# Strided attention in tiles of 36 tokens over four parts of TensorE's array, and weight slots at multiples of 128 bytes

## The chip, the cores and the metric

The kernel runs on one core of one Trainium2 chip. The metric is the device time of one execution in microseconds (us); the time of a kernel is the median of its runs. TensorE (PE) multiplies matrices, VectorE (DVE) and ScalarE (ACT) work elementwise, GpSimd (POOL) builds masks, SyncE (SP) issues nearly all DMA transfers.

## The reference

Inputs q, k, v have the shape (4, 8, 576, 64): batch, heads, tokens, head dimension, in float32. Heads 0 to 3 are local, heads 4 to 7 strided:

```
rel = pos[:, None] - pos[None, :]
mask_local   = (rel >= 0) & (rel < 32)
mask_strided = (rel >= 0) & (pos[None, :] % 32 == pos[:, None] % 32)
scores = where(mask, (q @ k.T) / 8, -1e9);  attn = exp(scores - max) / (sum + 1e-9);  attn @ v
```

The 2304 tokens of the result (4 batches of 576, 512 channels) go through two layers: `g = h * tanh(softplus(h))` with `h = x @ w_in` (512 to 2048) and `g @ w_out` back to 512; then `max(x @ w1, x @ w2, x @ w3) @ w_out` with an inner size of 768. The weights come as 8-byte numbers; the kernel turns them into a high and a low 4-byte part itself.

In strided attention a token sees only tokens with the same number modulo 32, so the 576 tokens fall into 32 residues of 18 tokens. A tile takes some whole residues; the mask lets a token see only its own residue's earlier tokens.

## The kernel before, in words

**Planner.** `build_plan` describes all work as small pieces with an engine, an estimated cost, the buffers that it reads and writes, and a rank. `Plan.run` plays a list schedule over the engines and `settle` repeats it forward and backward; the order found is emitted as it is. So every change of a piece can move the order of all of the others. Where PE would idle the planner puts filler matmuls (`fill`, L839) in.

**Attention.** There are 16 groups, one for each batch and pair of heads (`hp`); `hp` 0 and 1 are local, 2 and 3 strided. q and k of batch 0 are loaded early and transposed on PE (L355, copied at L368 and L370); the others are loaded as 128-byte pieces and transposed by DVE (L329), which writes the tokens of strided heads in the order of the residues. v comes by `load_v`; strided: six transfers a group, in 256-byte pieces (L834). `unit` (L377) handles 3 local tiles of 64 queries and 96 keys, or 4 (at the end 3) strided tiles of 3 residues: 54 queries and keys, 11 tiles a group, the last with 36. For each unit, in one PSUM bank from start to end: scores of both heads (PE, L413; head 0 in the rows 0 to 53 of the bank, head 1 from row 64 on), mask and scale (DVE, L426), row maximum (DVE, L432), for each tile an exponential with its sum (ACT, L438), guard, reciprocal and normalising (DVE, L445 to L451), a transpose of each tile (PE, L458), copy to `pt` (ACT, L463), product with v (PE, L471), and the result as a high part (ACT, L489) and the rest (DVE, L493) written to `x` at every 32nd token. Five banks (`ATT_BANKS`) go round among the units. The tiles `s`, `st` and `pt` are rings of 5, 8 and 3.

**First layer.** Products of 288 tokens with the first four chunks of w_in (L516, "raw", into `hr`) need the attention of their batch alone and lie among the attention units of the later batches; the last two blocks of tokens (8 of the 32 units) must follow the last attention unit. Then L543 multiplies by the first four chunks of w_out, and for five blocks of tokens (four of 512, one of 256) the chunks f = 4 to 15 of w_in (L516) and w_out (L543) follow. **Second layer:** for each block and each f = 0 to 5, w1 to w3 (L590) and w_out2 (L615; here the weights are the moving operand). A matmul with high and low parts is done as three passes over four chunks, so a group has 12 instructions.

**Slots.** Converted weights (4 KB in each partition) lie in 5 slots `a`, 11 slots `x` (laid over attention's buffers once these are closed) and 8 slots `y` (in the right-hand region, laid over `hr`). The right-hand region is laid out from the top down: first one block with `ident`, `edge` (an unused tile of 32 bytes), `wt`, `h` and `ev`, and below it, in turn, the early buffers, `hr` and the y slots. As laid out, every a and x slot begins at a multiple of 128 bytes and every y slot 64 bytes past one (the lowest at 168128 = 1313 x 128 + 64). By the order in which slots are freed, the y slots hold the chunks f = 10 to 13 of w_in and w_out in the first layer, and in the second six of the 18 chunks of w1 to w3 and two of the six of w_out2.

Of the kernel before, what the change touches and what calls it, by code (L numbers as in the profile page):

```python
# [19 lines left out]
P = 128  # L20
# [14 lines left out]
RES = 3  # L35
ATT_BANKS = ("a0", "a1", "a2", "acc1", "acc2")
RAW_BANKS = ("h0", "acc3")
# [152 lines left out]
def build_plan(k, B, H, S, D, DM, FF, FF2, wide):  # L190
# [110 lines left out]
    unit_tiles = {True: ((0, 1, 2), (3, 4, 5), (6, 7, 8)), False: ((0, 1, 2, 3), (4, 5, 6, 7), (8, 9, 10))}  # L301
    per_batch = 3 * H // 2
# [8 lines left out]
    def attention():  # L311
        n = 0
        for i, (b, hp) in enumerate(pairs):
            local = hp < 2
            r = i % 2
            rv = i if i < RING["v"] + 2 else i % RING["v"]
            rk0 = unit_rank(n)
            lr = rk0 - 8 if b else -200 + i
            if not b:
                early_qk(i, b, hp, local, r, rk0, lr)  # L320
            for nm in ("q", "k") if b else ():
                for g in range(4):
                    add("qk_load", "sp", S * PACKET[128], (lambda g=g, nm=nm, b=b, hp=hp, r=r: k.load_qk(nm, g, b, hp, k.raw(nm, r))),
                        writes=[("raw", nm, r, g)], rank=lr)

                def tr(nm=nm, r=r, local=local):
                    t = k.qkT(nm, r)
                    tv = t.rearrange("p (j r) -> p j r", r=STRIDE) if local else t.rearrange("p (r j) -> p j r", j=NJ)
                    nc.vector.transpose(out=tv, in_=k.raw(nm, r))  # L329

                add("tr", "dve", 669, tr, reads=[("raw", nm, r, g) for g in range(4)], writes=[("qT", nm, r)], rank=rk0 - 0.5)
            vparts = k.v_parts(hp)
            for j in range(vparts):
                v_cost = PACKET[256] * (LK * (2 if j == 0 else NL - 1) if local else NJ * (NS - (j % RES == RES - 1)))
                add("v_load", "sp", v_cost, (lambda j=j, b=b, hp=hp, rv=rv: k.load_v(j, b, hp, k.v(rv))),
                    writes=[("v", rv, j_) for j_ in range(j, 2 * RES, vparts)], rank=lr + 0.5)
            for u, tiles in enumerate(unit_tiles[local]):
                unit(n, i, u, tiles, b, hp, local, r, rv)
                n += 1
            if i == H // 2 - 1:  # L340
                add("hrpool", "dve", 0, k.open_hrpool, writes=[("earlypool",)], rank=-1)

    def early_qk(i, b, hp, local, r, rk0, lr):
# [5 lines left out]
        for j in range(2):  # L349
            for nm in ("q", "k"):  # L350
# [9 lines left out]
                def copy(nm=nm, j=j, tag=tag):  # L360
                    t, src = k.qkT(nm, r), k.bank(tag)[:, :half]
                    if local:
                        t = t[:, half * j:half * (j + 1)]
                    else:
                        t = t.rearrange("p (r j) -> p r j", j=NJ)[:, :, NJ // 2 * j:NJ // 2 * (j + 1)]
                        src = src.rearrange("p (j r) -> p r j", r=STRIDE)
# [10 lines left out]
    def unit(n, i, u, tiles, b, hp, local, r, rv):  # L377
# [5 lines left out]
        tag = ATT_BANKS[n % len(ATT_BANKS)]  # L383
        bk = ("bank", tag)
# [24 lines left out]
        for j, tl in enumerate(tiles):  # L409
            def scores(j=j, tl=tl):  # L410
                kw = LK if local else width(tl)
                for h in range(2):
                    nc.tensor.matmul(  # L413
                        ps()[LQ * h:LQ * h + width(tl), j * K:j * K + kw],
                        lhsT=cols("q", h, tl), rhs=cols("k", h, tl), start=True, stop=True,
                    )
            add("scores", "pe", 212 if local else 142, scores, reads=[("qT", "q", r), ("qT", "k", r)], writes=[bk], rank=rk, cols=4 * (K if local else width(tl)))

        def mask():
# [4 lines left out]
            else:  # L424
                m = k.m_first[:, 1, :].unsqueeze(1).broadcast_to([rows, nt, K])
            nc.vector.scalar_tensor_tensor(  # L426
                out=sv(), in0=ps()[:rows, :nt * K].rearrange("p (n c) -> p n c", c=K),
# [6 lines left out]
        add("mask", "dve", dve(nt * K), mask, reads=[bk], writes=[sb, *sk], rank=rk)  # L434
# [31 lines left out]
        for j, tl in enumerate(tiles):  # L466
# [9 lines left out]
            add("av", "pe", 160, av, reads=[pk] + [("earlypool",)] * (rv >= RING["v"]) + [("v", rv, j_) for j_ in range(2 * RES)], writes=[bk], rank=rk, cols=8 * width(tl) * K / P)  # L476
# [19 lines left out]
        add("a_lo", "dve", dve(nt * M), lo, reads=[bk, xhi, *at], writes=[xlo], rank=rk)  # L496

# [187 lines left out]
def sparse_attention_moe_kernel(  # L685
# [34 lines left out]
    upper.tile([P, 8], F32, name="edge")  # L720
# [16 lines left out]
    s_t = many(atc, "s", [P, 3 * LK])  # L737
    st_t = many(atc, "st", [P, 8])
# [3 lines left out]
    v_t = many(atc, "v", [P, 2, NS, D])  # L742
    v_t += [early_pool.tile([P, 2, NS, D], F32, name=f"v{i}") for i in range(RING["v"], RING["v"] + 2)]
# [8 lines left out]
    def build_masks():  # L752
# [8 lines left out]
        for h in range(2):  # L761
            half = m_res[LQ * h:LQ * (h + 1)].rearrange("p (r j) -> p r j", j=NJ)
            select(half, [[-NJ, RES], [-1, NJ]], 0, 1)
            select(half, [[NJ, RES], [0, NJ]], NJ - 1, -1)
# [52 lines left out]
    def load_v(j, b, hp, t):  # L817
# [12 lines left out]
        else:  # L830
            h, r = divmod(j, RES)
            vr = v[b, 2 * hp + h].rearrange("(j r) d -> j r d", r=STRIDE)
            n = len(range(r, STRIDE, RES))
            nc.sync.dma_start(out=t[NJ * r:NJ * (r + 1), h, :n, :], in_=vr[:, r::RES, :])  # L834
# [18 lines left out]
    with tc.manual_schedule():  # L853
# [5 lines left out]
        build_masks()  # L859
        for emit in order:  # L860
# [30 lines left out]
```

## Time and profile before

| | |
|---|---|
| median of 3 runs | 807.09 us (807.07 to 807.59) |
| profiled execution | 807.78 us; span of its instructions 806.0 us |
| PE busy | 797.0 us (99%), 5017 matmul instructions; 9 tenths or more in 39 of 40 slices |
| DVE busy | 360.7 us (45%) |
| ACT busy | 320.9 us (40%) |
| POOL busy | 4.4 us |
| DMA | 59.66 MB, 119,690 packets, of which 91,984 under 512 bytes |
| granted TensorE clock | 1.00 throughout |

The span reaches from the first to the last instruction. Busy time counts the time in which an instruction of the engine is under way; matmuls are pipelined and overlap, so that a busy PE may still have room. The chain of waits follows the run back from its last instruction to whatever released each step; its pieces say how long a group of instructions held up the end. A small float32 matmul of the attention appears as two PE instructions.

### The profile page before, as it was taken

The numbers are of one execution on the slowest core, as the hardware profiler recorded it, in microseconds if no ns is written. First come the engines' busy times: TensorE is split into PE (matmuls) and PEld (weight loads), VectorE is DVE, ScalarE is ACT, GpSimd is POOL, SyncE is SP. The second block draws the span as 40 slices with busy tenths as digits, with TensorE's granted clock in tenths as the row PEclk, the third lists the DMA queues.
The fourth block names the chain that finished last, engine by engine and source line by source line (L and its number), as shares of the span: only waits on it lengthen the run. The fifth ranks groups of instructions, "written<-read, shape, count | busy, mean of one in ns | idle before, by whom it ended". The sixth has DMA issues, their size and how long they took to land.

```text
span 806.0 us, 12605 instructions
## 1 busy us (share of the span) xinstructions
PE 797.0 (99%) x5017; PEld 669.3 (83%) x5017; DVE 360.7 (45%) x769; ACT 320.9 (40%) x839; POOL 4.4 (1%) x22
## 2 busy tenths in 40 slices
PE   9999999999999999999999999999999999999998
PEld 7878888988888888888888899888888888888897
DVE  6988886895931311311321179981212211122222
ACT  5978878997732322312322257630110110110111
POOL 2000000000000000000000000000000000000000
PEclk9999999999999999999999999999999999999999
DMA  9877750944900100100010079200100010010010
GB/s 206 157 152 132 135 102 22 349 148 170 326 0 1 53 0 1 53 0 1 1 52 0 1 227 322 105 1 0 53 1 0 16 38 1 0 53 1 0 53 27
DMA packets 119690, 59.66 MB, mean 74 GB/s; under 512 B 91984, under 2 KB 110416, under 8 KB 119632
## 3 DMA queue, kind: packets, MB, share of 16 engines
q1 hardware_dynamic: 118448, 58.57, 26.5%
q8 instruction: 39, 0.64, 0.3%
q10 hardware_dynamic: 1184, 0.30, 0.2%
q14 instruction: 19, 0.16, 0.1%
HBM read 49.41 MB, written 9.44 MB: 73 GB/s over the span
## 4 chain that ended last, share of the span: by engine, by line
PE 92%; DMA 3%; ACT 2%; DVE 2%; issue 1%; SPq 0%; DVEq 0%; ACTq 0%
PE bank_acc L543 24%; PE bank_a L590 21%; PE bank_a L516 13%; PE bank_acc L615 9%; PE bank_h L516 7%; PE bank_h L590 7%; PE bank_acc L516 3%; PE bank_a L413 2%; PE bank_a L471 1%; DMA wslot<-in_moe_w_dram 1%; PE bank_a L458 1%; DMA wslot<-in_moe_w_out_dram 1%; PE bank_acc L413 1%; ACT s L438 1%; PE bank_acc L471 1%; PE bank_acc L458 1%
## 5 line engine op out<-in xcount | busy, mean ns | idle before, releaser
L543 PE MATMUL bank_acc<-g,wslot 128*128 128x512 f32 (+1 forms) x960 | 205.4, 370 | 1.4 <-ACT g L537 1.0
L543 PEld LDWEIGHTS bank_acc<-g,wslot 128*128 128x128 f32 x960 | 168.3, 188 | 33.7 <-ACT g L537 1.2
L590 PE MATMUL bank_a<-x,wslot 128*128 128x512 f32 (+1 forms) x816 | 174.7, 369 | 0.0
L590 PEld LDWEIGHTS bank_a<-x,wslot 128*128 128x128 f32 x816 | 142.3, 188 | 26.9
L538 DVE TENSOR_TENSOR g<-h,g 128x512 fp32r<-128x512 f32 (+1 forms) x80 | 51.1, 639 | 194.8 <-ACT g L537 194.8
L516 PE MATMUL bank_a<-x,wslot 128*128 128x512 f32 (+1 forms) x540 | 117.2, 369 | 0.0
L516 PEld LDWEIGHTS bank_a<-x,wslot 128*128 128x128 f32 x540 | 94.5, 188 | 17.9
L599 DVE TENSOR_TENSOR h<-bank_a,h 128x512 f32<-128x512 f32 (+1 forms) x46 | 29.2, 635 | 138.9 <-PE bank_a L590 138.9
L615 PE MATMUL bank_acc<-wslot,g 128*128 128x512 f32 x324 | 78.8, 391 | 0.0
L516 PE MATMUL bank_h<-x,wslot 128*128 128x288 f32 (+2 forms) x372 | 74.5, 339 | 0.0
L615 PEld LDWEIGHTS bank_acc<-wslot,g 128*128 128x128 f32 x324 | 60.5, 188 | 12.8
L535 ACT ACTIVATE h<-bank_a 128x512 f32<-128x512 f32 (+1 forms) x45 | 25.0, 555 | 109.8 <-PE bank_a L516 109.8
L516 PEld LDWEIGHTS bank_h<-x,wslot 128*128 128x128 f32 x372 | 58.5, 188 | 7.4
L601 ACT ACTIVATE g<-h 128x512 fp32r<-128x512 f32 (+1 forms) x30 | 17.7, 589 | 116.1 <-DVE h L599 116.1
L590 PE MATMUL bank_h<-x,wslot 128*128 128x512 f32 (+1 forms) x264 | 58.8, 371 | 0.0
L438 ACT ACTIVATE s<-s,st 118x54 f32<-118x54 f32 (+1 forms) x160 | 55.5, 352 | 7.2 <-DVE st L432 6.9
L590 PEld LDWEIGHTS bank_h<-x,wslot 128*128 128x128 f32 x264 | 46.7, 188 | 9.0
L537 ACT CAST g<-h 128x512 fp32r<-128x512 f32 (+1 forms) x80 | 46.3, 579 | 4.5 <-PE bank_acc L543 2.7
L253 ACT ACTIVATE wt<-wslot 128x512 f32<-128x512 f32 x56 | 37.9, 678 | 22.7 <-DVE wslot L281 9.7
L277 ACT CAST wslot<-wt 128x512 fp32r<-128x512 f32 x56 | 34.5, 621 | 15.3 <-DVE wt L267 15.1
L281 DVE TENSOR_TENSOR wslot<-wt,wslot 128x512 fp32r<-128x512 f32 x56 | 38.6, 692 | 3.4 <-ACT wslot L277 3.4
L596 ACT COPY h<-bank_a 128x512 f32<-128x512 f32 (+1 forms) x22 | 12.0, 548 | 69.8 <-PE bank_a L590 69.8
(71 smaller groups left out, 680.4 us busy)
## 6 DMA issues: line engine op xcount, KB each, us to landing
wslot<-in_moe_w_out_dram SPq DMA_DIRECT2D x22, 512.0 KB
wslot<-in_moe_w_dram SPq DMA_DIRECT2D x18, 512.0 KB
wslot<-in_moe_w_in_dram SPq DMA_DIRECT2D x16, 512.0 KB
out_dram<-wt SPq DMA_DIRECT2D x18, 256.0 KB
x2p<-ev SPq DMA_DIRECT2D x16, 256.0 KB
ev<-x2p SPq DMA_DIRECT2D x16, 256.0 KB
rawq<-in_q_dram SPq DMA_DIRECT2D x48, 72.0 KB
rawk<-in_k_dram SPq DMA_DIRECT2D x48, 72.0 KB
```

Source lines behind the costliest of these rows:

```text
L253: nc.scalar.mul(k.wt(r2).bitcast(F32), k.words(slot)[1].bitcast(F32), 2.0 ** -111)
L277: nc.scalar.copy(out=k.open_slot(slot)[:, 0, :], in_=k.wt(r2).bitcast(F32))
L281: nc.vector.tensor_tensor(out=s[:, 1, :], in0=k.wt(r2).bitcast(F32), in1=s[:, 0, :], op=ALU.subtract)
L438: nc.scalar.activation(sv()[:, j, :], sv()[:, j, :], AF.Exp, bias=mx()[:, j:j + 1], accum_out=dn()[:, j:j + 1],)
L516: nc.tensor.matmul(k.bank(hb)[:, :n], lhsT=wap(("in", f), a, c), rhs=k.x[:, q, c, t0:t0 + n], start=(c == 0 and m == 0), stop=(c == KC - 1 ...
L535: add(name, "act", act(n, psum=not stored), lambda: nc.scalar.activation(Hh(), src(), AF.Mish, scale=W_SCALE), reads=sread, writes=[HK], r ...
L537: add("gh", "act", act(n), lambda: nc.scalar.copy(out=g()[:, 0, :n], in_=Hh()), reads=[HK], writes=[G0], rank=s)
L538: add("gl", "dve", dve(n), lambda: nc.vector.tensor_tensor(out=g()[:, 1, :n], in0=Hh(), in1=g()[:, 0, :n], op=ALU.subtract), reads=[HK, G0 ...
L543: nc.tensor.matmul(k.bank(f"acc{c}")[:, :n], lhsT=wap(("out", f), a, c), rhs=g()[:, q, :n], start=(first and m == 0), stop=(last and m == 2),)
L590: nc.tensor.matmul(k.bank(hb)[:, :n], lhsT=wap((w_, f), a, c), rhs=k.x[:, q, c, t0:t0 + n], start=(c == 0 and m == 0), stop=(c == KC - 1 a ...
L599: add("m2", "dve", dve(n), (lambda hb=hb: nc.vector.tensor_tensor(out=m_(), in0=k.bank(hb)[:, :n], in1=m_(), op=ALU.max)), reads=[("bank", ...
L615: nc.tensor.matmul(k.bank(ab)[:], lhsT=k.g(rg)[:, a, c * P:(c + 1) * P], rhs=t[:, q, :], start=(f == 0 and m == 0), stop=(f == F2C - 1 and ...
```

## The change

Strided units get a function of their own, `pair_unit`. A tile now has 2 residues (36 tokens), 16 tiles a group. A tile of the first half (residues a * 16 + n with n below 8) and one of the second half (n from 8 on) form a pair: for head h and half par, the scores stand in the bank `ins[par]` at row 64 * (h xor par), so that the four small matmuls of a pair use four different quarters of the array; one transpose turns both halves of a pair at once, and the products with v take rows 0 to 35 or 64 to 99 of v, by half, and go to the bank `outs[par]`. A unit has 4 pairs, a group 2 units. Scores of all units are written to `a0` and `a1`, transposes and results of all strided units to `a2` and `acc1`; local units now take turns at a0 and a1 for their scores and at a2, acc1 and acc2 for the rest. The exponential is one instruction over 288 elements after a subtraction of the maximum, and its sum a reduction on DVE; there are two masks, two high and two low parts for a unit, one for each half. In q the order of a tile's tokens is (residue, j), in k and v (j, residue), which lets v of a tile group be loaded as 36 rows of 2 KB. `s` becomes 2 KB in each partition and is cleared once by GpSimd. `edge` grows from 32 to 96 bytes, which moves the base of that block, and with it the early buffers, `hr` and the y slots, down by 64 bytes; wt, h and ev stay where they are.

```diff
-RES = 3
+RES = 2
+VKEYS = 12
+ATT_PAIRS = (("a0", "a1"), ("a2", "acc1"))
+IN_BANKS, OUT_BANKS = ATT_BANKS[:2], ATT_BANKS[2:]
@@ attention
-    unit_tiles = {True: ((0, 1, 2), (3, 4, 5), (6, 7, 8)), False: ((0, 1, 2, 3), (4, 5, 6, 7), (8, 9, 10))}
-    per_batch = 3 * H // 2
+    unit_tiles = {True: ((0, 1, 2), (3, 4, 5), (6, 7, 8)), False: ((0, 1, 2, 3), (4, 5, 6, 7))}
+    per_batch = 5 * H // 4
...
-                    tv = t.rearrange("p (j r) -> p j r", r=STRIDE) if local else t.rearrange("p (r j) -> p j r", j=NJ)
+                    if local:
+                        t = t.rearrange("p (j r) -> p j r", r=STRIDE)
+                    else:
+                        t = in_tile(t, nm).rearrange("p n a j -> p j a n")
...
-                unit(n, i, u, tiles, b, hp, local, r, rv)
+                (unit if local else pair_unit)(n, i, u, tiles, b, hp, local, r, rv)
+    def in_tile(t, nm):
+        return t.rearrange("p (n a j) -> p n a j" if nm == "q" else "p (n j a) -> p n a j", a=RES, j=NJ)
@@ unit
-        tag = ATT_BANKS[n % len(ATT_BANKS)]
-        bk = ("bank", tag)
+        tin, tag = IN_BANKS[n % len(IN_BANKS)], OUT_BANKS[n % len(OUT_BANKS)]
+        ik, bk = ("bank", tin), ("bank", tag)
@@ pair_unit (new)
+        for j, tl in enumerate(tiles):
+            for par in range(2):
+                def scores(j=j, tl=tl, par=par):
+                    for h in range(2):
+                        o = LQ * (h ^ par)
+                        nc.tensor.matmul(
+                            k.bank(ins[par])[o:o + K, j * K:(j + 1) * K],
+                            lhsT=qk("q", h, NS // 2 * par + tl), rhs=qk("k", h, NS // 2 * par + tl), start=True, stop=True,
+                        )
+        for par in range(2):
+            def mask(par=par):
+                nc.vector.scalar_tensor_tensor(
+                    out=sv()[:, par::2, :], in0=k.bank(ins[par])[:rows, :nt * K].rearrange("p (n c) -> p n c", c=K), scalar=SCALE,
+                    in1=k.m_res[:rows].unsqueeze(1).broadcast_to([rows, nt, K]), op0=ALU.mult, op1=ALU.add,
+                )
...
+        (DVE: rowmax, sub; ACT: one exponential; DVE: sum, guard, recip, norm, each over 2 * nt * K elements)
+                nc.tensor.transpose(
+                    k.bank(outs[0])[:rows, j * P:j * P + rows], k.buf(sb)[:rows, j * P:j * P + rows], k.ident[:rows, :rows]
+                )
...
+                    for h in range(2):
+                        c = j * P + LQ * (h ^ par)
+                        nc.tensor.matmul(
+                            k.bank(outs[par])[D * h:D * (h + 1), j * K:(j + 1) * K],
+                            lhsT=k.v(rv)[o:o + K, h, tl, :], rhs=k.buf(pb)[o:o + K, c:c + K], start=True, stop=True,
+                        )
+        (for each par: high part on ACT, low part on DVE, nt * K elements)
@@ buffers
-    upper.tile([P, 8], F32, name="edge")
+    upper.tile([P, 24], F32, name="edge")
-    s_t = many(atc, "s", [P, 3 * LK])
-    st_t = many(atc, "st", [P, 8])
+    s_t = many(atc, "s", [P, 4 * P])
+    st_t = many(atc, "st", [P, 16])
-    v_t = many(atc, "v", [P, 2, NS, D])
+    v_t = many(atc, "v", [P, 2, NL, D])
@@ load_v
-            nc.sync.dma_start(out=t[NJ * r:NJ * (r + 1), h, :n, :], in_=vr[:, r::RES, :])
+            nc.sync.dma_start(
+                out=t[o:o + RES * NJ, h, :NS // 2, :].rearrange("p n d -> p (n d)"),
+                in_=v[b, 2 * hp + h].rearrange("(p n) d -> p (n d)", n=NS)[:, n * par:n * (par + 1)],
+            )
@@ start
+        for t in s_t:
+            nc.gpsimd.memset(t[:], 0.0)
```

## Rows read from the trace of the kernel before

**Rows 1.** Windows: busy us (instructions) of each engine, clock, DMA share, GB/s.
```profile
core 0: us, PE busy (x) PEld busy (x) DVE busy (x) ACT busy (x) POOL busy (x), PEclk, DMA share, GB/s
20.00:40.00 20.00, 19.87 (x309) 16.72 (x307) 19.75 (x67) 18.96 (x82) 0.00 (x0) 1.00 0.89 156
60.00:140.00 80.00, 79.90 (x1104) 67.49 (x1104) 65.23 (x198) 64.23 (x277) 0.00 (x0) 1.00 0.54 99
```

**Rows 2.** Waits of PE, whole run (us, times, longest), and PE's filler matmuls.
```profile
PE bank_acc L839 <- DVE x L855: 1.2, 1, 1.2
PE bank_acc L543 <- ACT g L537: 1.0, 1, 1.0
...
L839 PE MATMUL bank_acc<-x x61: 274/283/583, 1.2 to 144.2; 128*128 128x256 f32 x61
```

**Rows 3.** Chain of waits, first 60 us: start us, us, what.
```profile
26.18 1.00 ACT s L438 x6
...
39.39 8.63 DMA wslot<-in_moe_w_out_dram
```

**Rows 4.** Chain of waits, one block of the first layer.
```profile
351.69 5.44 PE bank_acc L543 x24
...
368.00 5.60 PE bank_a L516 x24
```

**Rows 5.** Chain of waits, one block of the second layer.
```profile
545.47 8.40 PE bank_a L590 x36
553.87 2.76 PE bank_acc L615 x12
```

**Rows 6.** Chain of waits, the 256-column block.
```profile
494.25 2.08 PE bank_a L516 x18
...
498.99 1.80 PE bank_a L516 x15
```

**Rows 7.** Chain of waits among attention units, and where L543 begins.
```profile
95.27 0.52 PE bank_a L458 x4
...
97.95 0.01 PE bank_acc L413
...
102.36 0.60 PE bank_acc L471 x16
...
103.95 0.64 PE bank_a L413 x12
...
113.84 0.50 PE bank_a L471 x12
...
128.38 0.54 PE bank_a L413 x16
...
138.54 0.40 PE bank_a L458 x4
...
154.07 6.14 PE bank_acc L543 x27
```

**Rows 8.** DVE's groups by shape: busy us, mean ns; the last row min/median/max.
```profile
L451 DVE TENSOR_TENSOR s<-s,st 128x288 f32<-128x288 f32 x24 | 10.8, 452 | 0.4
L493 DVE TENSOR_TENSOR x<-bank_a,x 128x216 fp32r<-128x216 f32 x10 | 5.4, 545 | 3.9 <-ACT x L489 3.7
L426 DVE SCALAR_TENSOR_TENSOR s<-bank_a,m_res 118x216 f32<-118x216 f32 x10 | 3.7, 373 | 1.5 <-PE bank_a L413 1.5
L448 DVE RECIPROCAL st<-st 118x4 f32<-118x4 f32 x16 | 2.7, 171 | 0.2
L493 DVE TENSOR_TENSOR x<-bank_a,x 128x144 fp32r<-128x144 f32 x5 | 2.1, 415 | 0.0
...
L329 DVE STREAM_TRANSPOSE qTq<-rawq x12: 744/1010/1252, 30.3 to 119.5; 128x576 f32<-128x576 f32 x12
```

**Rows 9.** ACT's groups by shape: busy us, mean ns.
```profile
L438 ACT ACTIVATE s<-s,st 118x54 f32<-118x54 f32 x88 | 29.1, 337 | 2.7 <-DVE st L432 2.4
L438 ACT ACTIVATION_READ_ACCUMULATOR s<-s,st 118x1 f32 x88 | 17.2, 195 | 0.0
```

More of the change, by code (lines that the diff above doesn't have):

```diff
@@ L327, in tr @@
                     t = k.qkT(nm, r)
-                    tv = t.rearrange("p (j r) -> p j r", r=STRIDE) if local else t.rearrange("p (r j) -> p j r", j=NJ)
-                    nc.vector.transpose(out=tv, in_=k.raw(nm, r))
+                    src = k.raw(nm, r)
+                    if local:
+                        t = t.rearrange("p (j r) -> p j r", r=STRIDE)
+                    else:
+                        t = in_tile(t, nm).rearrange("p n a j -> p j a n")
+                    nc.vector.transpose(out=t, in_=src)
                 add("tr", "dve", 669, tr, reads=[("raw", nm, r, g) for g in range(4)], writes=[("qT", nm, r)], rank=rk0 - 0.5)
-            vparts = k.v_parts(hp)
+            vparts = 3 if local else 4
             for j in range(vparts):
-                v_cost = PACKET[256] * (LK * (2 if j == 0 else NL - 1) if local else NJ * (NS - (j % RES == RES - 1)))
+                v_cost = PACKET[256] * LK * (2 if j == 0 else NL - 1) if local else 300
                 add("v_load", "sp", v_cost, (lambda j=j, b=b, hp=hp, rv=rv: k.load_v(j, b, hp, k.v(rv))),
-                    writes=[("v", rv, j_) for j_ in range(j, 2 * RES, vparts)], rank=lr + 0.5)
+                    writes=[("v", rv, j_) for j_ in range(j, VKEYS, vparts)], rank=lr + 0.5)
             for u, tiles in enumerate(unit_tiles[local]):
-                unit(n, i, u, tiles, b, hp, local, r, rv)
+                (unit if local else pair_unit)(n, i, u, tiles, b, hp, local, r, rv)
                 n += 1
@@ L413, in scores @@
                     nc.tensor.matmul(
-                        ps()[LQ * h:LQ * h + width(tl), j * K:j * K + kw],
+                        k.bank(tin)[LQ * h:LQ * h + width(tl), j * K:j * K + kw],
                         lhsT=cols("q", h, tl), rhs=cols("k", h, tl), start=True, stop=True,
                     )
-            add("scores", "pe", 212 if local else 142, scores, reads=[("qT", "q", r), ("qT", "k", r)], writes=[bk], rank=rk, cols=4 * (K if local else width(tl)))
+            add("scores", "pe", 212 if local else 142, scores, reads=[("qT", "q", r), ("qT", "k", r)], writes=[ik], rank=rk, cols=4 * (K if local else width(tl)))
         def mask():
@@ L426, in mask @@
             nc.vector.scalar_tensor_tensor(
-                out=sv(), in0=ps()[:rows, :nt * K].rearrange("p (n c) -> p n c", c=K),
+                out=sv(), in0=k.bank(tin)[:rows, :nt * K].rearrange("p (n c) -> p n c", c=K),
                 scalar=SCALE, in1=m, op0=ALU.mult, op1=ALU.add,
@@ L475, in av @@
                     )
-            add("av", "pe", 160, av, reads=[pk] + [("earlypool",)] * (rv >= RING["v"]) + [("v", rv, j_) for j_ in range(2 * RES)], writes=[bk], rank=rk, cols=8 * width(tl) * K / P)
+            add("av", "pe", 160, av, reads=[pk] + [("earlypool",)] * (rv >= RING["v"]) + [("v", rv, j_) for j_ in range(VKEYS)], writes=[bk], rank=rk, cols=8 * width(tl) * K / P)
         def io(part):
@@ L741, in sparse_attention_moe_kernel @@
     qT_t = {nm: many(atc, "qT", [P, S], suffix=nm) for nm in "qk"}
-    v_t = many(atc, "v", [P, 2, NS, D])
-    v_t += [early_pool.tile([P, 2, NS, D], F32, name=f"v{i}") for i in range(RING["v"], RING["v"] + 2)]
+    v_t = many(atc, "v", [P, 2, NL, D])
+    v_t += [early_pool.tile([P, 2, NL, D], F32, name=f"v{i}") for i in range(RING["v"], RING["v"] + 2)]
     m_first = atc.tile([P, 3, LK], F32, name="m_first")
@@ L761, in build_masks @@
         for h in range(2):
-            half = m_res[LQ * h:LQ * (h + 1)].rearrange("p (r j) -> p r j", j=NJ)
+            half = m_res[LQ * h:LQ * (h + 1)].rearrange("p (j r) -> p r j", j=NJ)
             select(half, [[-NJ, RES], [-1, NJ]], 0, 1)
@@ L830, in load_v @@
         else:
[L831 to L834 removed]
+            h, par = divmod(j, 2)
+            n = NS // 2 * D
+            o = LQ * par
+            nc.sync.dma_start(
+                out=t[o:o + RES * NJ, h, :NS // 2, :].rearrange("p n d -> p (n d)"),
+                in_=v[b, 2 * hp + h].rearrange("(p n) d -> p (n d)", n=NS)[:, n * par:n * (par + 1)],
+            )
     zero = x[:, 0, KC - 1, NT - FILL:]
```

60 lines of the change are left out of this document (57 added, 3 removed).

## The prediction

> **What bounds the kernel now.** I read the windows of engine time first, then TensorE's waits, the chain of waits by stretch, and the groups of instructions by shape. The reader is to look in each for one thing: which engine has no idle time left, and what stands in the chain there. The windows [rows 1] split the run in three. To about 59 us TensorE (PE) has slack: 61 filler matmuls, nearly all of them there, keep its clock up [rows 2], VectorE (DVE) is busy 19.75 of 20 us and ScalarE (ACT) 18.96 between 20 and 40 us, and the chain runs through ACT's exponentials and one weight load of 8.63 us [rows 3]. From 59 to 154 us attention units lie between the 288-column matmuls of the first layer; PE is busy nearly without a break and the chain is PE's. From 154 us on PE's busy tenths are 9 in every slice but the last. Of PE's waits in the whole run the longest are 1.2 us, at the start, and 1.0 us, once, in the block of 256 columns [rows 2]; the granted clock is full (2.4 GHz) in every stretch [rows 1]. So what PE no longer has to do after 59 us comes off the end, as long as DVE and ACT follow; before 59 us it does not.
>
> **The change, part 1: the slots.** The larger `edge` moves the eight y slots by 64 bytes to multiples of 128. Do such slots cost anything now? The 24 matmuls with weights in a or x slots take 5.44 us in the chain, 24 with weights in y slots 5.60 us: 226.7 against 233.3 ns each, with the same 512 columns and the clock full [rows 4]. In each block, f = 10 to 13 is that slow stretch, and only it; the second layer shows the same, 8.40 us for 36 [rows 5]. Count: 8 weight chunks x 12 matmuls x 4 blocks of 512 columns = 384 in the first layer, 6 x 12 x 4 = 288 in the second, 672 x 6.6 ns = 4.4 us. Where the slot is the moving operand (two chunks of w_out2), twelve take 2.76 instead of 12 x 0.2267 = 2.72 us [rows 5], and some neighbours share it: another 0.5 us. The blocks of 256 columns I count at nothing: PE waits there for ACT anyway [rows 2]. Together 4.9, and I take 5.0 us. Bounds: 5.3 us if the neighbours share more than that; 0 if it is not the 64 bytes that make these slots slow but their place in the array, since no slot in that region lies at a multiple of 128 now. A loss has no row behind it: a and x slots lie at such multiples and are the fast ones.
>
> **Part 2: strided attention on PE.** Before, eight (batch, head pair) groups have 11 tiles each, 88 in all, 24 units. Every small matmul appears twice in the trace, so a tile of two heads has 4 PE instructions. The chain gives scores of four tiles 0.54 us, their four transposes 0.52, products with v 0.60 [rows 7]. With 0.40 and 0.45 us for the third, shorter units (estimates by columns), 16 x 0.54 + 8 x 0.40 = 11.8; 88 x 0.10 to 0.13 (0.40 us for four beside large matmuls, 0.52 between small ones) = 8.8 to 11.4; 16 x 0.60 + 8 x 0.45 = 13.2. In all about 35 us.
> After, there are 128 tiles of 36 tokens, and only 64 transposes, since two tiles share one. A score instruction takes 33.8 ns at 54 columns and 53.3 at 96 [rows 7], so about 25 at 36; one of v 37.5 at 54 and 41.7 at 64, so about 30. That is now, with two of the four parts of the array at work at a time. With no more overlap than that the sum is 128 x 0.10 + 128 x 0.12 + 64 x 0.10 = 34.6 us; with four parts at once, half of the first two terms, 20.5 us. So the saving lies between 0 and 14.5 us. The chain shows single instructions of two kinds of group released 0.01 us apart [rows 7], so issue is not what holds them to 25 ns, and I take three quarters of the way, 11 us. Six of the eight groups lie after 59 us: 8 us there.
> The Trainium skill, TensorEngine Tiling (Array Packing), section Instruction Overhead, speaks against this: about 60 cycles for each matmul however few its columns, so one shouldn't tile a dimension that is already small. At the full clock that is an estimated 25 ns an instruction; no row here shows a group with a mean below it, nor one so narrow by itself. By it 1,024 small instructions cost at least 25.6 us, with the transposes 32, and the saving would be 3 us: rival B.
>
> **Part 3: DVE, which pays.** Row durations per strided group [rows 8], before: masks 2 x 0.373 + 0.32, maxima the same, normalising the same, guards and reciprocals 3 x 2 x 0.17, subtractions for the low part 2 x 0.55 + 0.42: 5.7 us. After: four masks of 144 elements, some 0.30 each (0.373 less 72 elements at 1 ns each); maximum, subtraction, sum and normalising over 288 elements, two units x 4 x 0.45; 2 x 2 x 0.17; four low parts of 144 elements x 0.42: 7.1 us. That is +1.4 us a group, 11 us in all, 8.4 after 60 us. DVE is busy 65 of the 80 us from 60 to 140 [rows 1]; with 8.4 more it needs about 73.6. PE alone would bring that stretch down to 72. DVE at its best is 99% busy (20 to 40 us), so the stretch ends nearer 74.5 us: **I take 5.5 us, not 8**; DVE is late next. The strided write of a transposed q or k takes up to 1.25 us, a contiguous one 0.75 [rows 8]; the new layout's steps are of the same kind, 72 to 144 instead of 72 bytes, which I cost at 0, bounds 0 to 5 us for 12 of them.
>
> **Part 4: ACT, which gains.** Before, 11 x (0.337 + 0.195) = 5.9 us a group for exponentials [rows 9]. After: two over 288 elements without a sum, about 0.5 us each (estimate: 0.337 with 234 elements more, at DVE's 1 ns each). One copy to `pt` less and one high part more, all of them smaller, about cancel. So some 5 us a group go, 40 in all, but in the PE-bound stretch they were cover, so nothing by themselves; they keep ACT out of the way of what DVE and PE wait for. In the first 59 us, with two strided groups, ACT is on the chain and loses 10 us, while DVE, full from 20 to 40, gains 2.8: I take 0, with bounds of 3 us won (about half of the exponentials on that part of the chain are strided) and 2.8 lost.
>
> **Part 5: loads.** v comes in 4 transfers a group instead of 6, of 36 descriptors of 2 KB instead of pieces of 256 bytes. Loads of v name no long wait on PE [rows 2], so 0; less queueing could shorten the 8.63 us weight load by a microsecond at most. The five clears of `s` go to GpSimd, which is busy for 4.4 us in the whole run: 0, and 1 us at most.
>
> **Sum.** On the profiled execution (807.78 us, span 806.0): 5.0 for slots, 5.5 for attention, 797.3. The median of the runs shown, 807.09, is 0.69 below, so **796.6 us**.
>
> **Rivals.**
> A, slots gain nothing (place, not 64 bytes): 807.1 - 5.5 = 801.6. For it: all slow slots lie in one region. Against: with 256 columns the stretch that is two thirds y slots takes 2.08 us for 18 (116 ns each), one without them 1.80 for 15 (120) [rows 6], which is not how a generally slow region would look. 9%.
> B, small matmuls overlap no further than now: the bound of 34.6 us for PE holds, attention gains 0.3 us, and only the slots are left: 801.8. For it: the fastest groups shown still have a mean of 34 ns an instruction [rows 7]. Against: the halves sit in parts of the array that lay idle, in banks of their own. (By the floor that the Trainium skill's page above gives it would be 3 x 6/8, some 2 us, for attention: 799.8.) 24%.
> C, slower: all strided units now pass through the same four banks, and bank a2 is held from transposes to the low part. Now five banks rotate. Bare work of one pass is 0.5 for transposes, some 0.55 for the copy, 0.25 for v, 0.42 us for each of the two parts [rows 7 to 9], and four handovers of some 0.2: 3 us. 16 such, and 8 local units of some 3.5, are 76 us of the 130 that attention has, so there is room. It decides from a pass of about 6.5 us, if a2's readers queue behind other work on DVE (a transpose alone is 1 us [rows 8]): at 7 us, 16 x 7 + 8 x 3.5 + 10 at the start = 150 us instead of 141, +9 - 5 for slots: 811. 7%.
> D, better: four parts fully at once, and the chain of the first 59 us shorter by 3: 807.1 - 5 - 10.5 = 791.6. 12%.
> My forecast has 48%, its own range 794 to 799.
>
> **From these to the numbers.** The range 791 to 803 leaves out C and the tails of B and D. Faster by over 0.2% (1.6 us, about what a measurement can tell) holds for the forecast, D, A and nearly all of B: 0.89; within 0.2%: 0.05; slower: 0.06.
>
> **What would show it.** Slots: all groups of 24 with 512 columns at 5.44 us in the chain, no 5.60 left; blocks of 24 x 2.72 = 65.3 us. PE: eight score instructions (a tile of each half) in some 0.12 us, and the first long run of L543, at 154 us now [rows 7], from about 148.5. DVE: over 90% busy from 60 us to the last attention unit. Wrong: filler matmuls or waits of PE after 60 us, a DVE under 85% with PE idle (banks, C), or 5.60 us still there (A).

## The result, and the profile after

The changed kernel takes 811.63 us (median of 4 runs, 810.46 to 812.3) beside 807.08 us for the kernel before on the same chip: a ratio of 1.0055, 95% interval 1.0037 to 1.0072. It is slower by about 4.5 us. 796.6 us was forecast; both the direction and the range were wrong. The profiled execution took 810.46 us, its span 808.7 us (before 806.0); PE was busy for 801.4 us, DVE 366.5, ACT 298.2, POOL 6.7. The experiments below ran on several chips, where the kernel before took 807.1 to 808.1 us, so medians of different experiments compare to within some 1 us; each ratio is to the kernel before on the same chip.

In the changed kernel's line numbers the fillers are L938 (before L839), the strided scores L528, mask L536, row maximum L542, subtraction L544, exponential L546, sum L547, normalising L552, transposes L556, copy to `pt` L561, products with v L569, high and low parts L584 and L588; w_in's matmuls are L612 (L516), w_out's L639 (L543).

The stretches that answer to [rows 1], from the windows of the changed kernel:

```profile
20.00:40.00 20.00, 19.98 (x315) 18.13 (x309) 17.98 (x50) 9.92 (x26) 0.00 (x0) 1.00 0.89 180
60.00:140.00 80.00, 80.00 (x1279) 68.27 (x1278) 67.43 (x205) 47.29 (x161) 0.00 (x0) 1.00 0.52 99
```

ACT's busy time from 20 to 40 us has halved (18.96 to 9.92), and DVE, which took its work over, is not fuller but less full (19.75 to 17.98). From 60 to 140 us DVE is busy for 84%, not over 90%, and PE has no more room than before. The fillers, which answer to [rows 2], and the row of the kernel with the slots alone:

```profile
L938 PE MATMUL bank_acc<-x 128*128 128x256 f32 x147 | 24.7, 309 | 1.2 <-DVE x L954 1.2
```

```profile
L839 PE MATMUL bank_acc<-x 128*128 128x256 f32 x61 | 11.7, 332 | 1.2 <-DVE x L855 1.2
```

147 fillers instead of 61, and 129 of them instead of 53 before 60 us. The chain there, which answers to [rows 3], is from 7 us on PE alone, and the fillers are its largest part (25.7% of the first 62 us):

```profile
19.54 0.57 PE bank_a L528 x31
...
25.79 2.23 PE bank_acc L938 x17
...
31.41 0.27 PE bank_acc L569 x10
31.68 3.67 PE bank_acc L938 x29
35.35 0.57 PE bank_a L528 x31
...
45.80 1.88 PE bank_acc L938 x14
```

The unit whose scores start at 19.54 us reaches its products with v at 30.82 us; the sum of its steps' durations up to there is about 4.7 us. What lies between is seen on DVE's timeline, where a unit's steps alternate with the conversion of weights (L260, L264, L270, L284: 0.4 to 0.7 us each) and with the low parts of other units. The lines are of the unit after it:

```profile
30.14 0.44 DVE L542 TENSOR_REDUCE st<-s 100x8 f32<-100x288 f32 x1
30.50 0.68 DVE L270 SCALAR_TENSOR_TENSOR wt<-wslot,wt 128x512 uint32<-128x512 uint32 x1
31.10 0.45 DVE L544 TENSOR_TENSOR s<-s,st 100x288 f32<-100x288 f32 x1
...
32.26 0.41 DVE L260 TENSOR_SCALAR wt<-wt 128x512 uint32<-128x512 uint32 x1
32.60 0.67 DVE L284 TENSOR_TENSOR wslot<-wt,wslot 128x512 fp32r<-128x512 f32 x1
33.20 0.43 DVE L547 TENSOR_REDUCE st<-s 100x8 f32<-100x288 f32 x1
...
35.02 0.44 DVE L552 TENSOR_TENSOR s<-s,st 100x288 f32<-100x288 f32 x1
```

From row maximum to normalised scores this unit needs 5.3 us, with 2.1 us of work of its own on DVE. So batch 0's results come later. Its last strided low part, with the slots alone and in the changed kernel:

```profile
41.10 0.43 DVE L493 TENSOR_TENSOR x<-bank_a,x 128x144 fp32r<-128x144 f32 x1
```

```profile
51.18 0.40 DVE L588 TENSOR_TENSOR x<-bank_acc,x 128x144 fp32r<-128x144 f32 x1
```

That is 10 us later, and by 60 us PE has done 42 matmuls with w_in instead of 76. The slots, which answer to [rows 4] and [rows 5], from the chain in the first layer and in the second:

```profile
347.58 5.44 PE bank_acc L639 x24
353.02 5.44 PE bank_a L612 x24
...
374.79 5.44 PE bank_a L612 x24
```

```profile
550.38 8.16 PE bank_a L686 x36
558.54 2.72 PE bank_acc L711 x12
```

No 5.60, 8.40 or 2.76 is left. The attention, which answers to [rows 7] and [rows 8], from the chain and from DVE's and ACT's groups:

```profile
69.50 0.40 PE bank_a L528 x16
71.30 0.35 PE bank_a L556 x4
...
75.80 0.59 PE bank_acc L569 x16
...
161.67 13.40 PE bank_acc L639 x59
```

```profile
L536 DVE SCALAR_TENSOR_TENSOR s<-bank_a,m_res 100x144 f32<-100x144 f32 x32 | 9.5, 297 | 4.4 <-PE bank_a L528 4.1
L544 DVE TENSOR_TENSOR s<-s,st 100x288 f32<-100x288 f32 x16 | 7.1, 442 | 0.0
L588 DVE TENSOR_TENSOR x<-bank_a,x 128x144 fp32r<-128x144 f32 x16 | 6.8, 423 | 9.1 <-ACT x L584 9.0
L336 DVE STREAM_TRANSPOSE qTq<-rawq 128x576 f32<-128x576 f32 x12 | 11.9, 994 | 0.0
```

```profile
L546 ACT ACTIVATE s<-s 100x288 f32<-100x288 f32 x16 | 7.1, 446 | 3.6 <-DVE s L544 3.6
```

Where a half's 16 score instructions stand alone they take 0.40 us (25 ns each), and 16 with v 0.59 us (37 ns): no faster than the 25 and 30 ns that the prediction gave for no further overlap. Where the two halves' runs follow each other and mix in part, 31 take 0.57 us (18 ns), as in the chain above. The first long run of w_out's matmuls starts at 161.67 us; it was at 154.07 before and forecast for 148.5.

To compare the kernels I split PE's time up to that run: each matmul lasts to the start of the next, but at most 0.3 us, and the rest is pause. The fillers of the whole run lie in this stretch, most of them before 60 us.

| kernel (profiled execution), us | run starts | fillers | pauses | strided small matmuls | from there to the end |
|---|---|---|---|---|---|
| before | 153.9 | 10.6 | 2.8 | 34.8 | 652.1 |
| changed | 161.5 | 22.0 | 1.3 | 34.2 | 647.2 |
| slots alone | 151.1 | 10.4 | 1.9 | 34.8 | 646.9 |
| slots, changed softmax | 162.7 | 16.0 | 5.3 | 34.7 | 646.5 |
| slots, changed softmax in batch 0 | 167.3 | 14.5 | 7.8 | 35.7 | 646.9 |
| slots, changed softmax in batches 1 to 3 | 155.9 | 10.3 | 4.4 | 35.6 | 647.4 |
| changed, other costs in the plan | 162.2 | 14.4 | 4.1 | 35.0 | 646.7 |
| changed, pairs in one piece | 151.4 | 17.3 | 3.6 | 24.7 | 647.2 |
| changed, no maximum | 154.4 | 16.3 | 1.7 | 34.0 | 648.2 |
| best (last experiment) | 146.8 | 13.1 | 4.8 | 23.7 | 647.8 |

So of the profiled difference of +2.7 us, -4.9 come after the run's start (slots), +9.9 are fillers and pauses before it (23.3 against 13.4), and what is left of PE's work there, strided small matmuls included, gives -2.3. From 20 to 60 us PE is busy for 39.98 of 40 us in the changed kernel, so some of the fillers may hold up work and not only fill a gap; no run leaves them out.

### The profile page after: what moved, and what is told of

Read it like the earlier page. It is cut to its first block, busy times and chain, and to the rows that moved or that the text cites. A ratio compares the mean times of both kernels' runs of the same rounds, so it can differ in the third digit from the quotient of the medians.

```text
span 808.7 us, 13222 instructions
## 1 busy us (share of the span) xinstructions
PE 801.4 (99%) x5399; PEld 680.6 (84%) x5399; DVE 366.5 (45%) x785; ACT 298.2 (37%) x679; POOL 6.7 (1%) x27
## 4 chain that ended last, share of the span: by engine, by line
PE 94%; DMA 3%; DVE 1%; ACT 1%; issue 0%; SPq 0%; ACTq 0%
PE bank_acc L639 22%; PE bank_a L686 21%; PE bank_a L612 12%; PE bank_acc L711 9%; PE bank_h L612 8%; PE bank_h L686 7%; PE bank_acc L612 4%; PE bank_acc L938 2%; PE bank_a L423 2%; DMA wslot<-in_moe_w_dram 1%; PE bank_a L528 1%; PE bank_acc L481 1%; PE bank_a L569 1%; PE bank_acc L569 1%; PE bank_a L556 1%; PE bank_acc L468 1%
## 5 line engine op out<-in xcount | busy, mean ns | idle before, releaser
L639 PE MATMUL bank_acc<-g,wslot 128*128 128x512 f32 (+1 forms) x960 | 204.4, 369 | 1.1 <-DVE g L634 0.7
L639 PEld LDWEIGHTS bank_acc<-g,wslot 128*128 128x128 f32 x960 | 168.1, 188 | 32.6 <-DVE g L634 1.8
L612 PE MATMUL bank_a<-x,wslot 128*128 128x512 f32 (+1 forms) x540 | 116.2, 368 | 0.0
L612 PEld LDWEIGHTS bank_a<-x,wslot 128*128 128x128 f32 x540 | 94.6, 189 | 16.8
L612 PE MATMUL bank_h<-x,wslot 128*128 128x288 f32 (+2 forms) x372 | 74.9, 338 | 0.0
L711 PEld LDWEIGHTS bank_acc<-wslot,g 128*128 128x128 f32 x324 | 60.4, 188 | 12.3
L612 PEld LDWEIGHTS bank_h<-x,wslot 128*128 128x128 f32 x372 | 58.7, 188 | 7.4 <-ACT qTq L378 0.2
L284 DVE TENSOR_TENSOR wslot<-wt,wslot 128x512 fp32r<-128x512 f32 x56 | 38.1, 683 | 1.6 <-ACT wslot L280 1.5
L270 DVE SCALAR_TENSOR_TENSOR wt<-wslot,wt 128x512 uint32<-128x512 uint32 x56 | 38.1, 682 | 0.1
L264 DVE SCALAR_TENSOR_TENSOR wt<-wslot,wt 128x512 uint32<-128x512 uint32 x56 | 38.0, 683 | 0.2
```

The lines of the kernel that those rows point to most:

```text
L264: nc.vector.scalar_tensor_tensor(out=t, in0=k.words(slot)[1], scalar=0x80000000, in1=t, op0=ALU.bitwise_and, op1=ALU.bitwise_or)
L270: nc.vector.scalar_tensor_tensor(out=t, in0=k.words(slot)[0], scalar=29, in1=t, op0=ALU.logical_shift_right, op1=ALU.bitwise_or)
L284: nc.vector.tensor_tensor(out=s[:, 1, :], in0=k.wt(r2).bitcast(F32), in1=s[:, 0, :], op=ALU.subtract)
L612: nc.tensor.matmul(k.bank(hb)[:, :n], lhsT=wap(("in", f), a, c), rhs=k.x[:, q, c, t0:t0 + n], start=(c == 0 and m == 0), stop=(c == KC - 1 ...
L639: nc.tensor.matmul(k.bank(f"acc{c}")[:, :n], lhsT=wap(("out", f), a, c), rhs=g()[:, q, :n], start=(first and m == 0), stop=(last and m == 2),)
L711: nc.tensor.matmul(k.bank(ab)[:], lhsT=k.g(rg)[:, a, c * P:(c + 1) * P], rhs=t[:, q, :], start=(f == 0 and m == 0), stop=(f == F2C - 1 and ...
```

## The experiments

Three theories at the start, numbered as the expectations number them. Theory 1: the planner's costs for the small matmuls are too low, so it leaves batch 0's attention late. Theory 2: the strided units of batch 0 come late in themselves, since the softmax moved from ACT to DVE; the first products with w_in wait for batch 0, and fillers take the time. Theory 3: the halves of a pair do not meet on the array, because the plan issues them as separate pieces, and the small matmuls cost PE too much. Rivals were the shared banks (C) and the slots (A).

**The two halves of the change, each by itself.**

```diff
(before, slots alone)
-    upper.tile([P, 8], F32, name="edge")
+    upper.tile([P, 24], F32, name="edge")
(changed, old slots)
-    upper.tile([P, 24], F32, name="edge")
+    upper.tile([P, 8], F32, name="edge")
```

> The kernel before with the edge tile of 96 bytes alone, so only the y slots move to multiples of 128 bytes. If the 64 bytes are what makes their matmuls slow: 24 matmuls of 512 columns take 5.44 us everywhere, and the time falls by 4.9 us (the changed kernel's stretch from the first long run of w_out matmuls to the end is 647.0 us instead of 651.9): 802.2 us. If it is their place in the array: 807.1, and the 5.60 us stay.

> The changed kernel with the edge tile back at 32 bytes, so the attention alone is changed. If the two parts add up: 811.6 + 4.9 = 816.5 us, the first long run of w_out matmuls near 161.7 us as in the changed kernel. If the slots did something inside the attention too (ident, two v tiles and the early buffers move with them), it differs from 816.5 by over 1 us.

Slots alone: 801.27 us, ratio 0.9917 (0.9887 to 0.9947). Attention alone: 816.93 us, 1.0106 (1.0056 to 1.0156). The parts add up within 1 us: the slots give 5.3 us with the new attention (816.93 to 811.63) and 6.0 with the old; in the profiles the stretch from the run's start to the end gets shorter by 4.8 (652.0 to 647.2) and 5.2 us. Rival A is out, and the attention costs nearly 10 us where 5.5 of gain were forecast.

**Theories 1 and 3: other costs in the plan; both halves of a pair in one piece.**

```diff
(costs; the transpose's from 96 to 115 too)
-                add("scores", "pe", 38, scores, ...
+                add("scores", "pe", 100, scores, ...
-                add("av", "pe", 38, av, ...
+                add("av", "pe", 145, av, ...
(pairs in one piece; av alike, with 215)
-            for par in range(2):
-                def scores(j=j, tl=tl, par=par):
+            def scores(j=j, tl=tl):
+                for par in range(2):
...
+            add("scores", "pe", 145, scores, ..., writes=ik, rank=rk, cols=4 * K)
```

> The changed kernel with the planner's PE costs of the small strided pieces set to what the trace shows: 100 ns instead of 38 for scores, 145 instead of 38 for the products with v, 115 instead of 96 for a transpose. Only the order changes. Theory 1 (the planner took PE to have room and so left batch 0's attention late, with 15 us of fillers between 20 and 60 us): fillers there fall to about half, 805 us. Theory 2 (batch 0's strided units are slow in themselves, by DVE's longer chain): the same 811 us within 1.5. Theory 3 (the small matmuls cost PE too much): no change either.

> The changed kernel with both halves of a pair in one piece of 8 PE instructions, for scores and for the products with v, at planned costs of 145 and 215 ns, so that the four parts of the array are always offered work together. Theory 3: where the halves stand apart now a score instruction costs 25 ns (16 in 0.40 us) and together 18 (31 in 0.57), so PE's strided work falls from about 33 to 25 us, and 6 us of that come off: 805.5 us. Theory 1: some of the same, by the costs being nearer, 807. Theory 2: 811, since the first 60 us wait for DVE and not for PE.

Costs alone: 807.54 us, ratio 1.0006 (0.9978 to 1.0034). Pairs in one piece: 799.69 us, 0.9886 (0.9828 to 0.9944). The chain of the second:

```profile
64.69 0.41 PE bank_a L528 x32
65.11 0.60 PE bank_acc L612 x3
65.70 0.34 PE bank_a L556 x4
```

A unit's 32 score instructions take 0.41 us, 13 ns each, and the sum of the strided small matmuls falls from 34.2 to 24.7 us: the saving that the prediction expected is there once instructions for four different quarters of the array follow each other. Theory 3 holds, and the gain is larger than its 805.5 us. The costs by themselves, which the second kernel has too, leave the halves apart (35.0) and gain some 4 us by another order with fewer fillers, short of theory 1's 805. The early loss stays with the pairs in one piece: fillers and pauses are 20.9 us, against 12.3 with the slots alone, and batch 0's last strided result comes at 51.0 us.

**Theory 2: the changed softmax in the old attention.** The slots-alone kernel keeps its 54-token tiles; its strided units get DVE's subtraction and sum and one exponential for a unit.

```diff
-        for j in range(nt):
+        if local:            # second kernel: local or b > 0; third: local or b == 0
+          for j in range(nt):
             (exponential with bias and sum, one for each tile)
+        else:
+            add("sub", "dve", dve(nt * K), ...)
+            add("exps", "act", act(nt * K), ...)
+            add("sum", "dve", dve(nt * K), ...)
```

> The kernel before, with tiles of 54 tokens and its banks, and the slots moved as in e1 (801.3 us); only the softmax of strided units is done as in the changed kernel: DVE subtracts the maximum, one exponential on ACT, DVE sums. ACT loses some 37 us, DVE gains some 24 x 0.7 = 17 us. Theory 2a (the work moved from ACT to DVE is what makes batch 0's attention late): filler matmuls rise from 61 to about 90, the first long run of w_out matmuls comes 3 to 5 us later, 805 us. Theory 2b (it is the chain through shared banks or the load order, not DVE): 801 us or less, as ACT is freed.

> The kernel before with the aligned slots; the strided softmax (one subtraction and one sum on DVE, one exponential of the whole unit on ACT) as in the change, but in batch 0 alone; the other batches keep their exponentials with sums on ACT. With it in all batches the time was 813.3 us, with it in none 801.3. Theory L (the loss sits in the first 60 us: batch 0's units come late, the first products with w_in wait for them, filler matmuls or a lowered clock take PE's time): 811 to 813, with 80 to 95 filler matmuls. Theory S (the loss is DVE's extra load, spread over the run to 150 us): 802 to 805, since only a quarter of the units has it.

> The complement: the same softmax in batches 1 to 3 alone, batch 0 as before. Theory L: 801 to 803, some 61 filler matmuls, as with the slots alone. Theory S: 809 to 811, three quarters of the loss.

In all batches: 813.28 us, ratio 1.0055 (1.0034 to 1.0076). In batch 0 alone: 816.79 us, 1.0109 (1.0058 to 1.0159). In batches 1 to 3 alone: 803.39 us, 0.9948 (0.9923 to 0.9974). Slots alone had 0.9917, so batch 0 by itself costs some 15 us, more than all batches together, and the other three some 2. Batch 0's last strided result comes at 50.8 us with the changed softmax in batch 0, and at 45.7 with it in the others. Theory L holds in direction, with more loss than the 811 to 813 that it gave, as 813.28 is more than theory 2a's 805. In these old tiles the loss sits in the first 60 us, and DVE's added work after 60 us is nearly free. Each edit moves the plan's order too; edits that change no instruction moved the time by 4 to 5 us at most (the costs above, the names below), so that order alone has not been seen to do 15. Part of it is the clock. The window of the kernel with batch 0 alone, and of the one with the slots alone:

```profile
40.00:60.00 20.00, 16.50 (x138) 13.00 (x137) 11.22 (x34) 10.36 (x38) 0.00 (x0) 0.66 0.63 130
```

```profile
40.00:60.00 20.00, 19.78 (x239) 16.02 (x239) 19.25 (x54) 16.36 (x67) 0.00 (x0) 1.00 0.82 147
```

PE pauses (once for 3.4 us, for `pt`) and has a mean granted clock of 0.66 in this stretch, between its levels of 1.2 and 2.4 GHz; 138 matmuls go through instead of 239. In the changed kernel itself the clock is full from 20 us on (0.91 before): there it is the fillers that take the time.

The opposite move was run too, in the kernel with the pairs in one piece: an exponential with bias and sum on ACT for each of the 8 blocks of a unit, no subtraction and no sum on DVE.

```diff
-        add("sub", "dve", ...)
-        add("exps", "act", act(2 * nt * K), ...)
-        add("sum", "dve", ...)
+        for j in range(2 * nt):
+            add("exps", "act", act(K, ptr=True) + 93, (exponential with bias and sum of block j), ...)
```

Theory 2a expected 796 us of it, theory 2b 800 to 803. It took 805.79 us, ratio 0.9961 (0.9944 to 0.9979), so it was slower than with the softmax on DVE (799.69), and batch 0's last strided result came at 52.3 us, no earlier than the 51.0 there. What it returns is not the attention's result, for a reason that I did not find, so its time is a hint and no more. ACT has 128 such exponentials there, 88 in the kernel before, and is busy for 19.14 of the 20 us from 20 to 40. That the softmax's place is what makes batch 0 late in the new tiles is therefore not shown.

**Fewer steps on DVE, or one elsewhere.** The first two leave out row maximum and subtraction (the exponentials are of the plain scores), in all strided units and in batch 0's; the third gives batch 0's subtractions to GpSimd.

```diff
-        add("rowmax", "dve", ...)
-        add("sub", "dve", ..., nc.vector.tensor_tensor(...))
(batch 0 alone: both under "if b:")
(third)
+        on = "pool" if b == 0 else "dve"
+        add("sub", on, ..., (nc.gpsimd if on == "pool" else nc.vector).tensor_tensor(...))
```

> The changed kernel without the row maximum and its subtraction in strided units (these two of DVE's steps are left out, some 0.9 us for a unit, so the exponentials are of the plain scores); the small matmuls are issued as in the change. If batch 0's units are late because each has a long sequence of DVE steps, the filler matmuls before 60 us fall from 20 to some 12 us and the time from 811.6 to 803 to 806. Rival, the small matmuls' order on PE alone keeps them late: 809 to 812.

> The changed kernel without the row maximum and its subtraction (left out, some 0.9 us of DVE for a unit) in the four strided units of batch 0 alone. Left out in all sixteen, the time was 804.5 us against 811.6. If the whole loss sits in batch 0: 804 to 806. If it is spread over the batches: 809 to 810.

> The changed kernel with one of DVE's steps, the subtraction of the maximum (100 x 288), done by GpSimd in the four strided units of batch 0. DVE loses 4 x 0.45 us of work; each unit's own sequence gets longer, if GpSimd takes longer than DVE, which no row shows yet. If DVE's load in the first 60 us is what makes batch 0 late: 808 to 810. If the length of each unit's sequence does it: 811.5 to 814.

No maximum: 804.52 us, ratio 0.9957 (0.9937 to 0.9978). None in batch 0: 809.21, 1.0016 (0.9996 to 1.0035). GpSimd: 808.51, 1.0001 (0.9984 to 1.0018). The first falls as was expected. The second is where "spread over the batches" was expected: without the two steps in batch 0 some 2 to 3 us are gained, without them in the other twelve units too some 5 more. Batch 0's last strided result comes at 49.7 us in the second and at 45.9 in the first, although batch 0's own steps are the same in both, so what the other units put on DVE, or the order that follows from it, counts as well. GpSimd's subtraction takes 740 ns against DVE's 442, so the units' sequence grew, and still 3 to 4 us were gained, as DVE's load would have it.

**Load or length.** One more DVE instruction beside each strided unit of batch 0 (442 ns, read by nobody), or one more GpSimd step within it (955 ns).

```diff
(load)
+        if b == 0:
+            add("extra", "dve", dve(288), (a maximum over ident into edge), reads=[mk], writes=[("edge",)], rank=rk)
(length)
+        if b == 0:
+            add("extra", "pool", 700, (s = s + m_res), reads=[mk], writes=[sb, mk], rank=rk)
```

> The changed kernel with one more DVE instruction in each of the four strided units of batch 0: a maximum over 288 elements that nothing reads, some 0.44 us, ready together with the subtraction. No unit's own sequence needs it; DVE has 1.8 us more to do before 60 us. If DVE's load makes batch 0 late: 813 to 815 (taking 1.8 us away gave 3.1). If the length of a unit's sequence does: 811 to 812, as the changed kernel.

> The changed kernel with one more step in the sequence of the same four units, on GpSimd, which is otherwise idle: the mask is added to the scores once more between row maximum and subtraction (it changes nothing in the result), 0.75 us a unit by the subtraction's time there. DVE has nothing more to do. If the length of the sequence makes batch 0 late: 813 to 815. If DVE's load does: 811 to 812.

Load: 812.01 us, ratio 1.0060 (1.0042 to 1.0077). Length: 811.85 us, 1.0058 (1.0039 to 1.0076). Neither moves the time: 1.8 us of load and 3.8 us of length, over four units, find room where DVE is 82 to 90% busy (20 to 40 us). So neither of the two alone is shown to explain the delay, and the gain with GpSimd is no larger than what another order of the plan gives (the costs alone gave 4 us). What makes batch 0 late in the changed kernel stays open. Shown is that it is late, by 10 us, and that in the old tiles the softmax's move in batch 0 alone makes it late. Untested is a rival in the plan: a batch now has 10 attention units instead of 12, which shifts their ranks against the other pieces.

**Banks and names.**

```diff
(on top of pairs in one piece)
-        ins, outs = ATT_PAIRS
+        ins, outs = ATT_PAIRS[0], (OUT_BANKS[0] if n % 2 else OUT_BANKS[2], OUT_BANKS[1])
(names: high and low parts of the two halves are waited for one by one)
-            xhi, xlo = ("xa", 0, b, hp, u), ("xa", 1, b, hp, u)
+            xhi, xlo = ("xa", 0, b, hp, u, par), ("xa", 1, b, hp, u, par)
```

> The joint kernel (e4, 799.7 us) with transposes and first-half results of strided units going alternately to a2 and acc2 instead of always to a2. My rival C (all strided units queue for one bank): fillers before 60 us fall by half and the time goes to 795. If the bank is not what they wait for: 799.7 within 1.

> The joint kernel (e4, 799.7 us) with separate planner keys for the high and low parts of the two halves, so that the planner no longer makes the second half's copy wait for the first half's subtraction. No instruction changes, only their order. If this false order is what makes batch 0's last units late: 797 us. Otherwise 799.7 within 1.

> The pairs' eight small matmuls issued together (799.7 alone), the transposes' bank alternating (798.3 with it), and the high and low parts of the two halves told apart in the plan (799.1 with it). Both theories: the gains of 1.4 and 0.6 add up, 797.7; below 796 would mean that the two halves' shared buffer name had hidden something while one bank served all transposes.

Banks: 798.33 us, ratio 0.9874 (0.9859 to 0.9888). Names: 799.07, 0.9877 (0.9861 to 0.9894). Both: 802.91, 0.9935 (0.9901 to 0.9968). One shared bank costs some 1 us, within the intervals, and with it alternating the fillers and pauses are no fewer (21.2 us against 20.9), tested with the pairs in one piece: rival C's mechanism is not what made the kernel slow, though its figure of 811 came close. The two together were expected at 797.7 and missed: among the ten runs, those with a mean granted clock of 0.999 or more took 798.9 to 801.9 us and those at 0.995 or less 803.9 to 808.1; in the profiled one, at 0.992, PE waits once for 2.4 us, for `pt`, and the granted clock is 0.75 from 40 to 60 us.

**The best version: pairs in one piece, alternating bank, subtraction on GpSimd** in all strided units, or in batch 0's.

> The version with pairs issued together and the transposes' bank alternating (798.3 us), with the subtraction on GpSimd in all sixteen strided units: 16 x 0.45 us less on DVE. If DVE's load is what is left: 794 to 797. If the length of the sequence counts: 798 to 801.

> The same with GpSimd's subtraction in batch 0 alone. If the load of the first 60 us is all that counts, as with all sixteen units, 794 to 797; if DVE is short after 60 us too, 1 to 2 us above that.

```diff
+        on = "pool" if b == 0 else "dve"     # the other: "pool" in all batches
```

All units: 800.49 us, ratio 0.9917 (0.9886 to 0.9948). Batch 0: 796.92 us, 0.9853 (0.9820 to 0.9886), 11 us below the kernel before, the fastest that I ran. That GpSimd does part of it isn't shown; the interval takes in the version without it. With the work in all batches on GpSimd the time rose instead of falling to the expected 794 to 797 (nine runs, 796.9 to 807.23 us), for which I have no shown reason. The window and GpSimd's row of the better one:

```profile
20.00:40.00 20.00, 18.61 (x362) 15.86 (x362) 19.81 (x58) 11.66 (x33) 3.31 (x4) 1.00 0.81 171
```

```profile
L545 POOL TENSOR_TENSOR s<-s,st 100x288 f32<-100x288 f32 x4 | 3.3, 828 | 25.0 <-PE bank_acc L481 12.9 <-DVE st L542 6.7 <-DVE st L552 5.4
```

DVE is nearly full there again, as in the kernel before [rows 1].

## Why the prediction was wrong

- **Slots, 5.0 us: right.** 6.0 measured alone, 5.3 with the new attention; every group of 24 is at 5.44 us.
- **Part 2, "I take three quarters of the way, 11 us": failed.** The kernel as issued saves 0.6 us (34.8 to 34.2), which is rival B's bound. The step reasoned from where the halves' operands lie on the array; that the plan holds them as separate pieces of one half each, and mostly plays one half's instructions before the other's, stands in the code and was not read as a condition. With the pairs in one piece the saving is 10.1 us (34.8 to 24.7), so the size was right for a kernel that was not the one predicted.
- **Parts 3 and 4, the first 59 us, "I take 0, with bounds of 3 us won ... and 2.8 lost": failed, by the most.** Fillers and pauses before w_out's first long run grew by 9.9 us. The bounds counted busy time of ACT (down 10) and DVE (up 2.8). But batch 0's units gate the products with w_in, and their wait is not a sum of busy times: DVE ended up less busy from 20 to 40 us, with the units' steps queued among conversions of weights, and batch 0's last strided result came 10 us later than with the slots alone. The changed softmax in batch 0 alone, in the old tiles, cost some 15 us; what does it in the new tiles stays open.
- **"DVE is late next" after 60 us: not so in this kernel.** 67.43 of 80 us, and PE without a pause. It comes nearer where PE has less to do: with the pairs in one piece DVE is busy for 20.00 of the 20 us from 60 to 80, and PE for 18.73.
- **DVE's and ACT's durations, transposes: right.** Masks 297 ns (0.30), 288 elements 435 to 448 (0.45), low parts 423 (0.42), stream transposes 994 ns against 1010. The exponential took 446 ns; "about 0.5 us" was not far off, but its own terms, 0.337 and 234 elements at 1 ns, add up to 0.57.
- **Rivals.** B had the PE term right, but its 801.8 took the early part at nothing. C had a figure near the result by a mechanism that the alternating bank shows to be worth some 1 us. The slower case that happened, a later batch 0, was in no rival. That the best version's 796.92 us is near the forecast is luck: its strided matmuls save 11 us, and fillers and pauses still take 4.5 us more than before.

## What to carry to other kernels

A saving from parts of the array working at once is a matter of issue order: look whether the instructions of the parts really follow each other one by one before it is counted. Where an engine's work is moved to another inside a dependent sequence, don't price it by busy times: find what waits for the end of the sequence, and test the move in that stretch alone. And fillers in a trace are slack only until something later needs the time: count them before and after, beside the clock.

## What was not expected of the hardware

- 32 small instructions over four quarters of the array take 0.41 us, 13 ns each, when they alternate; 16 over two quarters take 0.40 us, 25 ns each. By the Trainium skill, TensorEngine Tiling (Array Packing), section Instruction Overhead, with its some 60 cycles for each matmul, an estimated 25 ns would be the least; the trace shows half of that for each of its instructions. For each matmul as the kernel writes it, which shows as two instructions, it is 26 ns, so the figure would hold if it is meant for those.
- The subtraction over 100 x 288 elements took GpSimd 740 to 828 ns, DVE 442.
- Weights 64 bytes past a multiple of 128 cost 6.6 ns for each matmul of 512 columns (233.3 against 226.7 ns), and moving them took all of it away.
